# Full-width Z C v, one output pass for two batches, transposes by DMA and a laid-out gate in a Nystrom attention and gating kernel

## The chip, the cores and the metric

The kernel runs on one core of a Trainium2 chip. The metric is the device time of one execution in microseconds, taken several times; the "span" in a profile is the time from the first to the last instruction of the profiled execution, some 1.7 us less. For a program on one core "slow" says only that a run was more than 1.5% above the fastest run of the same kernel on that chip, so it also marks kernels whose own time varies.

## The reference

Eight batches of an attention with 32 landmarks per head, then a gated long convolution on the 512 channels.

```python
B, H, S, D = 8, 8, 576, 64;  m = 32
q_lm = q.reshape(B, H, m, S // m, D).mean(axis=3)
k_lm = k.reshape(B, H, m, S // m, D).mean(axis=3)
A = sm(q, k_lm); Bm = sm(q_lm, k_lm); C = sm(q_lm, k)      # softmax of scaled scores
Z = Bm^T / (norm1(Bm) * norminf(Bm) + 1e-6)
for _ in range(6): Z = 2 * Z - Z @ Bm @ Z
x = (A @ Z @ C @ v)                                        # then heads side by side
proj = x @ w_proj;  x1, x2, x3 = thirds of proj
y = x1 * irfft(rfft(x2) * rfft(filter)) * x3
out = y @ w_out
```

## The kernel before

A batch passes through six parts, each written as a generator: `front` (landmarks, the small matrix), `turns` (k and q turned so that the head dimension lies on partitions), `inverse` (six Newton steps), `back` (scores, exponentials, A, C v, Z C v), `gate` (DFT, filter, inverse DFT, products) and `project` (times w_out, and out). The parts that the argument needs:

```python
def turns(b):                       # batches 0 and 1: on TensorE
    ...
    mm(pt[:, u * R:(u + 1) * R], ..., ident[:R, :R], is_transpose=True, ...)
    (nc.scalar.copy if i == 1 else nc.vector.tensor_copy)(dst[...], pt[:, 0:8 * R])

def inverse(b):
    if b >= NPE:                    # NPE = 2: from batch 2 on by DMA, on the SP queue
        for src, dst in zip((kn, qn), tbufs[b % 2]):
            nc.sync.dma_start_transpose(dst[...], src[...])
    ...

def back(b):
    ...
    A = big.tile([R, NC, 256], F16, tag="A", name="A", bufs=1)
    ...
    for g in range(2):              # A turned on TensorE, evicted by VectorE
        pt = ktile("ptA", F16)
        for c in range(NC):
            mm(pt[:, c * R:(c + 1) * R], A[:, c, 128 * g:128 * g + 128],
               identh[:R, :R], is_transpose=True, start=True, stop=True)
        nc.vector.tensor_copy(AT[:, g, :], pt[:, :S])

def project(b):
    for i0 in range(0, 512, P):     # four passes of 128 rows
        po = wtile()
        for j in range(4):
            mm(po, y[:, j, i0:i0 + P], wout[:, j, :], start=(j == 0), stop=(j == 3))
        os = big.tile([P, Dm], F32, tag="os", name="os", bufs=4)
        nc.scalar.copy(os, po)
        store(i0, P, os)            # nc.sync.dma_start: the SP queue as well
        yield
    po = wtile()                    # the last 64 rows, in two column halves
    ...
    o2 = big.tile([P, 256], F32, tag="o2", name="o2", bufs=1)
    nc.vector.tensor_copy(o2, po[:, 0:256])
    ...                             # two stores
```

`tag` names a pool of `bufs` buffers: a tile waits until the oldest user of its pool is done. The steps of `project` of one batch are done inside the next batch's gate. Loads are issued by GpSimd on a queue of its own (they cast from float32).

The softmax here doesn't subtract the row's maximum and nothing guards it: scores larger than these inputs give would overflow.

## Time and profile before

The median of the runs was 240.9 us (three runs). I mark the start of each batch's gate by its first DFT matmul and name the time from one to the next "gate 0", "gate 1" and so on.

| window, us | to gate 0 | gate 0 | gate 1 | gate 2 | gate 3 | gate 4 | gate 5 | gate 6 | gate 7 and end |
|---|---|---|---|---|---|---|---|---|---|
| before | 33.7 | 32.2 | 28.8 | 25.7 | 24.3 | 24.5 | 22.8 | 21.2 | 28.3 |

A row of the windows view gives the stretch, its length, each engine's busy time with its number of instructions in brackets, and last the granted TensorE clock, the share of the DMA engines in use (it can pass 1, as below) and GB/s. The prediction shows these rows; TensorE is busy 99.5% of a steady window. One more row of that view will matter, gate 2 of the kernel before:

```profile
94.79:120.50 25.71, 25.50 (x330) 15.58 (x327) 21.91 (x56) 21.93 (x51) 3.65 (x5) 1.00 1.39 164
```

The DMA share of 1.39 says that the transfers are crowded there, and still TensorE is busy 25.5 of 25.7 us: nothing waits for them.

### The profile page before, as it was taken

What the parts mean: (1) busy time and instruction counts of PE and PEld (TensorE: products, weight loads), DVE (VectorE), ACT (ScalarE), POOL (GpSimd) and SP (SyncE); (2) the same over time, 40 slices, a digit from 0 to 9 for tenths busy, and PEclk for the clock granted to TensorE, in tenths of its full rate; (3) what the DMA queues carried; (4) which work ended last, traced back from release to release, by engine and by line L of the source; (5) the groups of instructions that cost most, each with busy time, mean ns of one, the idle gap of its engine ahead of it and who ended that gap; (6) DMA issues with size and microseconds to landing.
All of it is one profiled execution on the core that took longest, in us unless ns stands there. A gap on an engine that the chain in (4) does not pass through costs nothing.

```text
span 241.6 us, 6421 instructions
## 1 busy us (share of the span) xinstructions
PE 223.4 (92%) x2547; PEld 134.6 (56%) x2547; DVE 182.4 (75%) x478; ACT 185.8 (77%) x407; POOL 37.7 (16%) x62
## 2 busy tenths in 40 slices
PE   7959769999999999999999999999999999999980
PEld 3537434666665667645754576457645664554630
DVE  8936943579978989896879777977797789567540
ACT  8663525888879878888878888788878987898850
POOL 7962310012203321040032001100000000000000
PEclk9967965999999999999999999999999999999998
DMA  5999999949999999999999996995015004305115
GB/s 73 195 210 196 208 202 198 172 80 176 165 149 167 218 196 154 177 191 146 171 217 140 165 230 152 115 157 173 3 47 152 0 3 107 89 4 150 48 42 153
DMA packets 61998, 33.78 MB, mean 140 GB/s; under 512 B 42320, under 2 KB 57680, under 8 KB 61968
## 3 DMA queue, kind: packets, MB, share of 16 engines
q0 software_dynamic: 27536, 16.85, 53.7%
q1 hardware_dynamic: 34432, 16.52, 36.1%
q8 instruction: 20, 0.33, 0.6%
q14 instruction: 10, 0.08, 0.1%
HBM read 33.69 MB, written 9.44 MB: 178 GB/s over the span
## 4 chain that ended last, share of the span: by engine, by line
PE 78%; DVE 9%; ACT 9%; issue 1%; DVEq 0%; ACTq 0%
PE w L612 12%; PE w L680 11%; PE w L639 6%; PE w L568 6%; PE w L537 6%; PE w L547 5%; PE pc L385 4%; PE pv L421 4%; PE pn L362 3%; PE w L641 3%; PE pq L257 2%; PE ptA L460 2%; PE w L504 2%; PE w L583 2%; PE pk L247 2%; ACT EO L643 2%
## 5 line engine op out<-in xcount | busy, mean ns | idle before, releaser
L680 PE MATMUL w<-wout,y 128*128 128x512 bf16 x128 | 33.4, 380 | 0.4 <-DVE y L658 0.4
L612 PE MATMUL w<-AT,G 128*128 128x512 f16 x128 | 32.8, 380 | 0.2
L541 ACT CAST G<-w 128x512 bf16<-128x512 f32 x48 | 25.5, 597 | 4.0 <-PE w L537 3.9
L617 DVE TENSOR_TENSOR gt<-w,x 128x512 bf16<-128x512 f32 x32 | 21.6, 685 | 9.0 <-ACT x L615 5.0
L643 ACT CAST EO<-w 128x288 bf16<-128x288 f32 x64 | 24.1, 403 | 2.8 <-PE w L641 2.8
L682 ACT COPY os<-w 128x512 f32<-128x512 f32 x32 | 18.5, 589 | 8.9 <-PE w L680 8.3
L639 PE MATMUL w<-IV,Y 128*128 128x288 f16 x128 | 25.0, 286 | 0.3 <-ACT EO L643 0.3
L573 DVE TENSOR_TENSOR T<-X,HH 128x2048 bf16<-128x2048 bf16 x16 | 19.5, 1220 | 7.1 <-ACT X L570 6.4
L615 ACT CAST x<-w 128x512 bf16<-128x512 f32 x32 | 19.0, 599 | 2.9 <-PE w L612 2.4
L537 PE MATMUL w<-wproj,ZC 128*64 128x512 bf16 x96 | 19.4, 400 | 0.0
L547 PE MATMUL w<-F,AE 96*128 96x304 f16 x96 | 19.2, 313 | 0.1
L680 PEld LDWEIGHTS <-y 128*128 128x128 bf16 x128 | 11.0, 97 | 14.5 <-issue 4.2
L570 ACT CAST X<-w 128x512 bf16<-128x512 f32 x32 | 17.9, 592 | 1.4 <-PE w L568 0.9
L396 DVE TENSOR_REDUCE rA<-eA 96x16 f32<-96x512 bf16 x24 | 16.2, 677 | 3.0 <-ACT eA L388 2.8
L641 PE MATMUL w<-IV,Y 128*128 128x288 f16 x64 | 18.3, 286 | 0.0
L568 PE MATMUL w<-G,Ah 128*128 128x512 bf16 x64 | 18.0, 382 | 0.0
L612 PEld LDWEIGHTS <-G 128*128 128x128 bf16 x128 | 11.0, 97 | 12.5 <-ACT G L541 4.0
L366 ACT CAST RZ<-pn 128x256 f16<-128x256 f32 x40 | 15.4, 386 | 2.8 <-PE pn L362 1.8
L96 POOL DMA_DIRECT2D vb<-in_v_dram x16 | 10.8, 678 | 41.0 <-PE w L547 25.1
L549 ACT CAST Ah<-w 128x304 f16<-128x304 f32 x32 | 12.8, 421 | 4.3 <-PE w L547 4.2
L362 PE MATMUL pn<-RZ 128*128 128x160 f16 (+1 forms) x96 | 13.7, 223 | 2.3 <-DVE RZ L367 1.7
L729 PE MATMUL w<-zero 128*128 128x512 bf16 (+1 forms) x55 | 14.2, 398 | 1.4 <-DVE zero L138 1.4
(152 smaller groups left out, 472.4 us busy)
## 6 DMA issues: line engine op xcount, KB each, us to landing
kn<-in_k_dram POOLq DMA_DIRECT2D x8, 576.0 KB, 9.7
qn<-in_q_dram POOLq DMA_DIRECT2D x16, 288.0 KB, 11.5
vb<-in_v_dram POOLq DMA_DIRECT2D x16, 288.0 KB, 9.7
out_dram<-os SPq DMA_DIRECT2D x24, 192.0 KB, 2.5
out_dram<-os SPq DMA_DIRECT2D x16, 128.0 KB, 2.4
wproj<-in_moe_w_proj_dram POOLq DMA_DIRECT2D x3, 512.0 KB, 14.8
out_dram<-os SPq DMA_DIRECT2D x24, 64.0 KB, 2.1
out_dram<-o SPq DMA_DIRECT2D x16, 64.0 KB, 2.1
```

The source lines that it names most:

```text
L362: mm(pn2[:, g, lo:160], RZ[:, g, 0:128], RZ[:, g, lo:160], start=True, stop=True, skip_group_check=True)
L537: mm(pg[64 * pp:64 * pp + 64, :], part["ZC"][:, 2 * g + pp, :, :].rearrange("p h l -> p (h l)"), wparts[jb][:, 2 * g + pp, :], start=True, ...
L541: nc.scalar.copy(G[:, g, Dm * jb:Dm * (jb + 1)], pg)
L547: mm(pf[:, 0:TW], part["AE"][:, par, c, 128 * g:128 * g + 128], F[:, c, par, :], start=(c == 0), stop=(c == 2))
L568: mm(px, Ah[:, g, par, 128 * t:128 * t + 128], G[:, g, Dm:2 * Dm], start=(g == 0), stop=(g == 1))
L573: nc.vector.tensor_tensor(T, X.unsqueeze(2).to_broadcast([P, 2, 2, Dm]), HH[:, par], op=ALU.mult)
L612: mm(px, G[:, g, lo:lo + P], part["AT"][:, g, 0:512], start=(g == 0), stop=(g == 1))
L617: nc.vector.tensor_tensor(gt[:, j, 0:512], px, x1, op=ALU.mult)
L639: mm(pi[:, 0:HS], Y[:, par, t, P * j:P * j + P], IV[:, par, t, :], start=(t == 0), stop=False)
L641: mm(pi[:, 0:HS], Y2[:, P * (j % 2):P * (j % 2) + P], IV2[:, j // 2, par, :], start=False, stop=True)
L643: nc.scalar.copy(EO[:, par, j % 2], pi[:, 0:HS])
L680: mm(po, y[:, j, i0:i0 + P], wout[:, j, :], start=(j == 0), stop=(j == 3))
```

## The change

The intent is to take work off TensorE and to lay the rest out so that it never stands. Z C v comes out at full width because each head's C v has a zero half beside it; G is then made of eight small matmuls on 64x32 tiles, not four on 128x64. The tail frequencies and the last 64 output rows lose their column tiling (two batches share one pass). A's transposes, and those of batch 1's k and q, go to the DMA. The gate is woven in two phases with the side work at fixed places, and the tables are made between the steps of the first front.

```diff
-    NPE = 2
+    NPE = 1                       # k, q on TensorE for batch 0 only
+    NPA = 1                       # A on TensorE for batch 0 only
...
-        A = big.tile([R, NC, 256], F16, tag="A", name="A", bufs=1)
+        A = big.tile([R, 2, NC, P], F16, tag="A", name="A", bufs=1)
...
+        AT = big.tile([P, 2, S], F16, tag="AT", name="AT")
+        if b >= NPA:
+            nc.sync.dma_start_transpose(
+                AT.rearrange("p g (c r) -> p (g c) r", r=R), A.rearrange("p g c l -> p (g c l)"))
...
+            for pos in range(4):
+                for g in range(2):
+                    mm(pg[g][32 * pos:32 * pos + 32, :], part["ZC"][64 * g:64 * g + 64, pos, :],
+                       wparts[jb][64 * g:64 * g + 64, head(g, pos) // 2, :],
+                       start=True, stop=True, skip_group_check=True)
...
-        o2 = big.tile([P, 256], F32, tag="o2", name="o2", bufs=1)
-        nc.vector.tensor_copy(o2, po[:, 0:256])
+        if b % 2 == 1:
+            yl = lasts.pop(b // 2)
+            po = wtile()
+            for j in range(4):
+                mm(po, yl[:, j].rearrange("p e s -> p (e s)"), wout[:, j, :],
+                   start=(j == 0), stop=(j == 3))
+            o2 = big.tile([P, Dm], F32, tag="os", name="o2", bufs=4)
+            nc.vector.tensor_copy(o2, po)
...
+        for b in range(2, B):
+            g = gate(b, pending)
+            todo = [(g, 7, 0, 1)]
+            if b + 1 < B: todo.append((K_[b + 1], 9, 0, 1))
+            if b + 2 < B: todo.append((F_[b + 2], 8, 0, .9))
+            turns_dma(b + 2)
+            weave(*todo, end=False); run(*[(x[0], ALL) for x in todo[1:]])
+            vload(b + 2)
+            todo = [(g, 17, 0, 1)]
+            if b + 2 < B: todo += [(E_[b + 2], 6, 0, .9), (I_[b + 2], 6, 0, 1)]
+            weave(*todo)
+            loads(b + 3)
+            pending = project(b)
```

(The cuts leave out the layout of the tail tables, the zero halves, the start and the order of heads.)

## The prediction

> **What bounds the kernel now.** I read the page first, then cut the span into batches, then asked for the chain of waits inside one batch. The page:
>
> ```profile
> PE 223.4 (92%) x2547; PEld 134.6 (56%) x2547; DVE 182.4 (75%) x478; ACT 185.8 (77%) x407; POOL 37.7 (16%) x62
> PEclk9967965999999999999999999999999999999998
> DMA  5999999949999999999999996995015004305115
> PE 78%; DVE 9%; ACT 9%; issue 1%; DVEq 0%; ACTq 0%
> ```
>
> TensorE is busy 92% of 241.6 us and holds 78% of the chain that ended last. Averages mix the start with the steady part, so I marked where each batch's gate begins, by the first DFT matmul (line 547) of each, and asked for the windows between these marks:
>
> ```profile
> core 0: us, PE busy (x) PEld busy (x) DVE busy (x) ACT busy (x) POOL busy (x), PEclk, DMA share, GB/s
> 0.00:65.97 65.97, 56.10 (x626) 34.71 (x627) 47.49 (x145) 43.29 (x89) 23.14 (x42) 0.87 1.18 171
> ...
> 120.50:144.83 24.33, 24.13 (x291) 14.31 (x289) 19.44 (x51) 20.62 (x47) 3.64 (x5) 1.00 1.25 190
> 144.83:169.32 24.49, 24.36 (x298) 14.80 (x295) 19.76 (x52) 20.94 (x48) 1.33 (x2) 1.00 0.89 149
> ...
> 213.32:241.60 28.28, 21.08 (x154) 10.77 (x151) 12.86 (x23) 17.62 (x38) 0.00 (x0) 0.97 0.31 84
> ```
>
> In the steady batch TensorE is busy 24.36 of 24.49 us; ScalarE has 20.94 (86%), VectorE 19.76 (81%). So a steady batch is TensorE's, but ScalarE stands only 3.5 us below. The start is different: 65.97 us for one batch, with a granted clock of 0.87 and no engine full. Its chain runs through VectorE making the sine table (1.4 to 12.3 us), a table load on ScalarE, then a ladder of short steps.
>
> The rows that the change touches:
>
> ```profile
> L537 PE MATMUL w<-wproj,ZC 128*64 128x512 bf16 x96 | 19.4, 400 | 0.0
> L462 DVE COPY AT<-ptA 128x576 f16<-128x576 f16 x16 | 7.2, 447 | 3.9 <-PE ptA L460 3.9
> ...
> L583 PE MATMUL w<-G,Ah 128*32 128x256 bf16 x128 | 5.8, 276 | 0.0
> L688 PE MATMUL w<-wout,y 128*64 128x256 bf16 x64 | 5.4, 274 | 0.0
> ```
>
> Durations overlap here, so I took the time in the chain: in the batch from 142.7 to 167.2 us the chain gives line 537 8.2% of 24.49 us (2.0 us for 12 matmuls), line 583 2.2% (0.54 us for 16), line 460 2.1% (0.51 us for 12). Full matmuls of 512 columns stand at 0.86 us for four there, 215 ns each.
>
> **What the Trainium skill says.** "TensorE: Matmul & The Clock Gate", section "Back-to-back issue gap", gives N/2.4 + 2.5 ns for a warm matmul alone, 216 ns at N = 512. The trace agrees: 215 ns. The same page, "Part 3: Packing small matmuls", has small tiles in different row and column strips run side by side (nine tiles 6.32 times as fast as one by one). The trace shows it for columns alone: 16 matmuls of 256 columns on 32-wide tiles take 0.54 us where one by one would be 16 x 109 ns = 1.7 us. Rows and columns at once it does not show. "TensorEngine Tiling (Array Packing)", section "Key Properties", says that a change of tiling mode drains the engine: the four matmuls of line 537 stand at 0.55 us or more in the chain against 2 x 216 ns = 0.43. "VectorE: DVE Perf Modes", section "The three transpose paths", gives 390 ns on TensorE and 1309 ns by DMA for a 128x128 block, but TensorE pipelines: here twelve 96-column transposes take 0.51 us of chain, and the DMA's time is beside it.
>
> **The change, part by part, on TensorE in one steady batch.**
> 1. The transposes of A go to the DMA (all batches but the first): -0.51 us, and two VectorE copies, -0.89 us there.
> 2. G from ZC: four matmuls on 128x64 tiles become eight on 64x32 tiles, eight places at once. Ideal is one pass of 216 ns; with a drain and eight starts I take 0.40 us (an estimate) in place of 2.0/3 = 0.67 us. Three such parts: -0.8 us.
> 3. The tail frequencies: 16 tiled matmuls become two full ones, 2 x 0.216 = 0.43 against 0.54: -0.11 us. VectorE loses one instruction, line 592, 285 ns.
> 4. The last 64 rows: 8 half-width matmuls per batch (ideally 4 x 109 = 0.44 us, x64 in the row above) become 4 full ones per pair of batches, 0.43 us a pair: -0.22 us.
> 5. ZC wants 8 matmuls in place of 4 (about 30 ns each): +0.12. DFT tables are 320 wide, not 304: 12 x 16 / 2.4 = 80 ns: +0.08.
> Sum: -0.51 - 0.8 - 0.11 - 0.22 + 0.2 = -1.44 us, so 24.49 becomes about 23.05 us. ScalarE keeps all its evictions (20.9 us, 91% of that), so it should not bind yet, but half of its slack is gone. VectorE: -0.89 - 0.29 - 0.13 (ZC copy half as large) + 0.07 (y in two pieces) = 18.5 us.
>
> **The start.** Batch 1's k and q are no longer turned on TensorE: 48 transposes of 96 columns (2 us) and six evictions of 0.55 to 0.8 us leave the window before 66 us. The tables are made between the steps of the front, with the two constants and ScalarE fills after them put later: the first lm copy starts at 15.7 us now, while q arrives for the matmul at 10.5 us; I give 3 us for that. Batch 0 gets parts 2 to 5 (0.9 us), batch 1's back part 1. With the second half of gate 0 woven through batch 1's scores, inverse and batch 2's front, I estimate 1 us more. Together 65.97 becomes about 58.5 us.
>
> **The sum by windows** (now, then): to gate 1, 65.97, 58.5. Gate 1, 28.82, 27.5. Gate 2, 25.71, 24.0. Gates 3 and 4, 24.33 and 24.49, each 23.0. Gate 5, 22.80, 23.0, because the front of batch 7 is now done here, not earlier. Gate 6, 21.20, 18.7 (the scores of batch 7 have moved into gate 5). Gate 7 and the end, 28.28, 26.5 (-1.4 of TensorE, and ScalarE has 17.6 there, so nearly all counts). New total: 58.5 + 27.5 + 24.0 + 23.0 + 23.0 + 23.0 + 18.7 + 26.5 = 224.2 us of span. Span and measured median agree within 1 us before (241.6 and 240.9), so I say **224 us**, -7%.
>
> **Rivals.**
> *The DMA becomes the bound.* Its queues tell what moves:
>
> ```profile
> q0 software_dynamic: 27536, 16.85, 53.7%
> q1 hardware_dynamic: 34432, 16.52, 36.1%
> ...
> kT<-kn SPq DMA_TRANSPOSE x6, 10.9
> qT<-qn SPq DMA_TRANSPOSE x6, 9.3
> ```
>
> Before: 33.78 MB. Added: two transposes of 0.59 MB for batch 1 and seven of A, half as large each: 1.18 + 2.06 = 3.2 MB. Loads alone run at 202 GB/s (window 20 to 38 us), transposes alone at about 185 (46 to 50 us). 37.0 MB at 190 GB/s are 195 us of 224. For this rival: a steady batch moves 3 x 0.59 + 2 x 0.59 + 0.29 + 1.18 = 4.4 MB in 23 us, 192 GB/s, about what the DMA gives; and the stores wait in the same queue as the transposes, in order. Against it: now the last load is issued at 150 us with DMA share under 0.25 after 169 us, so there is slack at the end, and no compute engine waits for a transfer longer than 0.2 us after the start. If it holds, a batch costs 25 us and the total is 230 to 238.
> *ScalarE becomes the bound.* 20.94 us per batch plus small gaps is 21.5 to 22; TensorE at 23.05 is above. It binds only in gate 1, with two batches of exponentials: part of why I take only 1.3 us off there. If the weave puts evictions badly, a batch stays at 24: total 229.
> *The small tiles don't overlap.* If rows and columns together gave no more than columns do now, eight matmuls of 512 columns on four places cost 0.43 + 0.1 us and the gain of part 2 falls from 0.8 to 0.4 us: 227. If they ran one by one, 8 x 216 = 1.73 us, +3.2 us per batch and no gain at all: 249. The tiled matmuls in the trace speak against the last.
> *Better than counted.* TensorE's streaming columns in a batch sum to some 22.6 us by my count, so 1.9 us are stalls and drains; a weave that takes away half of them and a start that never drops to half clock (0.50 at 38 to 40 us) would give 214 to 217, where ScalarE stops it.
>
> **Range and chances.** 224, with 214 to 234 for 8 in 10: below lies the better weave, above the DMA or ScalarE. Faster by over 2% means under 236.1 us; only a saturated DMA or serial tiles take the result there. Faster 0.91, same 0.07, slower 0.02.
>
> **What would show it.** Steady gates 23 us apart with TensorE over 97% busy: the sum is right. TensorE under 93% with ScalarE over 95%: ScalarE binds. Waits of scores or of the factor matmuls on kT, qT or AT of many us: the DMA. G's matmuls: eight in under 0.45 us of chain, or not. The first lm copy near 12.5 us, and gate 1 near 58 us: the start is right. The prediction fails if DMA transposes land too late for the scores of batches 1 and 2, where loads still fill the engines, or if the woven order makes TensorE, which runs in order, stand behind an eviction.

## The result

The changed kernel took 254.8 us in the median of four runs (253.7 to 256.6) beside 242.4 for the kernel before: slower, with a ratio of 1.055 (95% interval 1.042 to 1.068). Ratios here are the mean time of one kernel's fast runs over that of the other's fast runs of the same rounds, so they are not quite the ratio of the medians. The predicted 224 us with its range of 214 to 234 was wrong, and on the wrong side of the kernel before.

The page of the changed kernel, the lines that answer to the first four of the prediction, and the row of TensorE's busy share:

```profile
PE 209.2 (82%) x2369; PEld 125.1 (49%) x2369; DVE 172.6 (68%) x460; ACT 185.4 (73%) x411; POOL 38.0 (15%) x62
PE   7868699179499699919139999999999999999990
PEclk9999889959979999976858999999999999999997
DMA  6999999999999899999992999989205203604116
PE 37%; DMA 29%; DVE 12%; ACT 11%; SPq 3%; issue 3%; POOL 2%; DVEq 0%; ACTq 0%
```

TensorE has 14 us less to do, as meant, but the chain that ended last is no longer TensorE's: 29% of it are transfers, which the same line of the kernel before does not list at all. The granted clock is at 5 to 7 tenths only in and just after the slices in which TensorE was busy for 1 to 4 tenths; the longest such stretch lies just before the middle of the span. The windows:

| window, us | to gate 0 | gate 0 | gate 1 | gate 2 | gate 3 | gate 4 | gate 5 | gate 6 | gate 7 and end |
|---|---|---|---|---|---|---|---|---|---|
| predicted | 58.5 for both | | 27.5 | 24.0 | 23.0 | 23.0 | 23.0 | 18.7 | 26.5 |
| after | 29.7 | 40.4 | 28.4 | 42.5 | 22.6 | 23.2 | 22.0 | 18.1 | 28.1 |

```profile
29.66:70.08 40.42, 30.00 (x381) 18.99 (x382) 24.95 (x77) 24.09 (x52) 4.43 (x6) 0.87 1.35 176
98.44:140.93 42.49, 27.57 (x308) 16.60 (x304) 22.42 (x59) 22.75 (x52) 3.63 (x5) 0.80 1.11 165
140.93:163.55 22.62, 21.70 (x281) 13.37 (x277) 18.76 (x50) 20.11 (x47) 3.65 (x5) 1.00 1.30 176
163.55:186.71 23.16, 22.41 (x286) 13.70 (x282) 19.43 (x51) 20.34 (x47) 1.33 (x2) 1.00 0.65 142
```

From gate 3 on the windows lie within 1.6 us of the prediction. The whole miss sits in two windows. Gate 0 ends at 70.1 us, not 58.5: 11.6 us. Gate 2 lasts 42.5 us, not 24: 18.5 us. Together 30.1 us, and 224.2 + 30.1 is 254.3; the span was 254.9. In both windows no engine is near full, so they are made of waits.

The waits of the changed kernel in gate 0 (who waited for whom: total us, times, longest):

```profile
PE pc L410 <- DMA qT<-qn: 8.9, 2, 6.7
```

and in gate 2 (some lines are left out):

```profile
DVE o L719 <- DMA out_dram<-os: 10.8, 1, 10.8
...
PE pn L386 <- DVE RZ L391: 9.4, 1, 9.4
...
DVE A L442 <- DMA AT<-A: 5.8, 1, 5.8
```

In gate 0 the scores of batch 1 wait 6.7 us for qT, now made by DMA, and those of batch 2 wait 2.3 us. In gate 2 VectorE first waits 5.8 us to write A, because the transpose that reads A's only buffer has not finished. Then it waits 10.8 us to write `o`, the last rows of two batches, because the pool of four `os` buffers has none free: a store has not landed. TensorE's 9.4 us are VectorE's wait handed on, since the Newton step that it needs stands behind that copy on VectorE, which did nothing else meanwhile. Why the store is late is seen on the SP queue (start, us, issue):

```profile
103.94 3.45 SPq L448 DMA_TRANSPOSE AT<-A  x1
107.55 3.21 SPq L360 DMA_TRANSPOSE qT<-qn  x1
110.87 7.14 SPq L360 DMA_TRANSPOSE kT<-kn  x1
118.10 1.00 SPq L700 DMA_DIRECT2D out_dram<-os  x2
119.20 5.98 SPq L448 DMA_TRANSPOSE AT<-A  x1
125.27 3.46 SPq L700 DMA_DIRECT2D out_dram<-os  x6
```

ScalarE had filled the first `os` buffer by 104 us. Its store was issued at 118.1 us, after A's transpose of batch 2 and both transposes of batch 5 (the fifth pair in the queue, of which batch 1's is the first; some of the expectations below call it batch 4's), and landed at about 129.4 us, when the chain lets VectorE go. Of the 25.4 us, 14.1 lie before the issue. The rest, 10.7 us to land for the last piece, is long too: the medians of such stores are 2.6 to 3.8 us by size. Batch 5's transposes were ahead of it on the same queue, and its kT landed at 127.4 us.

### The profile page after: what moved, and what is told of

It is laid out like the page before. It is cut to its first block, busy times and chain, and to the rows that moved or that the text cites. A ratio compares the mean times of both kernels' runs of the same rounds, so it can differ in the third digit from the quotient of the medians.

```text
span 254.9 us, 6078 instructions
## 1 busy us (share of the span) xinstructions
PE 209.2 (82%) x2369; PEld 125.1 (49%) x2369; DVE 172.6 (68%) x460; ACT 185.4 (73%) x411; POOL 38.0 (15%) x62
## 4 chain that ended last, share of the span: by engine, by line
PE 37%; DMA 29%; DVE 12%; ACT 11%; SPq 3%; issue 3%; POOL 2%; DVEq 0%; ACTq 0%
DMA qT<-qn 15%; PE w L707 6%; PE w L636 5%; DMA AT<-A 5%; DMA out_dram<-os 5%; PE w L575 5%; DMA kn<-in_k_dram 4%; PE w L663 4%; SPq L360 3%; PE pc L410 2%; ACT EO L667 2%; DVE T L606 2%; PE w L665 2%; PE w L564 2%; PE w L601 2%
## 5 line engine op out<-in xcount | busy, mean ns | idle before, releaser
L636 PE MATMUL w<-AT,G 128*128 128x512 f16 x128 | 34.8, 380 | 2.8 <-DMA AT<-A 2.2
L663 PE MATMUL w<-IV,Y 128*128 128x288 f16 x128 | 27.1, 301 | 0.0
L667 ACT CAST EO<-w 128x288 bf16<-128x288 f32 x64 | 24.2, 411 | 2.6 <-PE w L665 2.1
L568 ACT CAST G<-w 128x512 bf16<-128x512 f32 x48 | 25.1, 605 | 0.6 <-PE w L564 0.6
L709 ACT COPY os<-w 128x512 f32<-128x512 f32 x32 | 18.7, 595 | 8.4 <-PE w L707 8.4
L390 ACT CAST RZ<-pn 128x256 f16<-128x256 f32 x40 | 15.8, 394 | 10.9 <-PE pn L386 10.8
L413 ACT ACTIVATE eA<-pc 96x512 bf16<-96x512 f32 x24 | 15.0, 624 | 12.0 <-PE pc L410 12.0
L386 PE MATMUL pn<-RZ 128*128 128x160 f16 (+1 forms) x96 | 14.1, 229 | 11.4 <-DVE RZ L391 11.0
L639 ACT CAST x<-w 128x512 bf16<-128x512 f32 x32 | 19.7, 617 | 3.5 <-PE w L636 3.1
L707 PEld LDWEIGHTS <-y 128*128 128x128 bf16 x128 | 11.9, 99 | 15.8 <-issue 2.9
L575 PE MATMUL w<-F,AE 96*128 96x320 f16 x96 | 17.5, 325 | 2.1 <-DVE AE L475 2.1
L665 PE MATMUL w<-IV,Y 128*128 128x288 f16 x64 | 19.2, 300 | 0.0
L410 PE MATMUL pc<-lm,qT 128*128 128x64 bf16 x192 | 11.0, 201 | 9.7 <-DMA qT<-qn 8.9
L83 POOL DMA_DIRECT2D kn<-in_k_dram x8 | 6.5, 815 | 74.6 <-PE pk L269 28.1
L386 PEld LDWEIGHTS <-RZ 128*128 128x128 f16 x96 | 8.5, 98 | 17.9 <-issue 13.6
L601 PE MATMUL w<-G,Ah 128*128 128x512 bf16 x64 | 16.7, 380 | 0.0
L98 POOL DMA_DIRECT2D vb<-in_v_dram x16 | 10.8, 677 | 39.4 <-PE pv L458 33.2
## 6 DMA issues: line engine op xcount, KB each, us to landing
qn<-in_q_dram POOLq DMA_DIRECT2D x16, 288.0 KB, 12.5
```

The lines of the kernel that those rows point to most:

```text
L386: mm(pn2[:, g, lo:160], RZ[:, g, 0:128], RZ[:, g, lo:160], start=True, stop=True, skip_group_check=True)
L568: nc.scalar.copy(G[:, g, Dm * jb:Dm * (jb + 1)], pg[g])
L575: mm(pf[:, 0:TW], part["AE"][:, par, g, c, :], F[:, c].rearrange("p a x -> p (a x)")[:, TW * par:TW * par + TW], start=(c == 0), stop=(c = ...
L601: mm(px, Ah[:, g, o:o + P], G[:, g, Dm:2 * Dm], start=(g == 0), stop=(g == 1))
L636: mm(px, G[:, g, lo:lo + P], part["AT"][:, g, 0:512], start=(g == 0), stop=(g == 1))
L639: nc.scalar.copy(x1, px)
```

## The experiments

Twelve kernels ran. I began with two theories. **A, order:** single waits in the one in-order queue that carries stores and transposes. **B, bytes:** the transfers are at their limit until gate 3, so only the megabytes count. B looked good at first: from the windows (length times GB/s) the kernel before had moved 20.7 MB when its gate 3 began at 120.5 us, the changed one 24.3 MB at 140.9 us, and 3.6 MB at 180 GB/s are the 20 us of delay. After four runs I formed a third: **C**, two separate losses, batch 1's transposes in gate 0, and the shared output buffer behind a blocked queue in gate 2. The windows of all runs' profiled executions:

| kernel | to gate 0 | gate 0 | gate 1 | gate 2 | gate 3 | gate 4 | gate 5 | gate 6 | span |
|---|---|---|---|---|---|---|---|---|---|
| before | 33.7 | 32.2 | 28.8 | 25.7 | 24.3 | 24.5 | 22.8 | 21.2 | 241.6 |
| changed | 29.7 | 40.4 | 28.4 | 42.5 | 22.6 | 23.2 | 22.0 | 18.1 | 254.9 |
| e1 | 29.7 | 32.4 | 32.8 | 36.8 | 22.6 | 23.2 | 22.0 | 18.1 | 245.8 |
| e2 | 30.7 | 36.3 | 26.3 | 41.5 | 22.9 | 23.7 | 22.4 | 18.6 | 250.4 |
| e3 (slow) | 30.8 | 32.4 | 26.5 | 38.1 | 22.9 | 23.7 | 22.4 | 18.6 | 243.5 |
| e4 | 30.8 | 40.9 | 28.1 | 30.1 | 22.6 | 23.2 | 22.0 | 18.1 | 244.0 |
| e5 | 30.7 | 32.4 | 26.5 | 25.6 | 22.9 | 24.5 | 22.3 | 18.6 | 231.5 |
| e6 | 29.7 | 32.4 | 26.0 | 31.1 | 22.6 | 23.2 | 22.0 | 18.1 | 233.3 |
| e7 | 29.7 | 39.8 | 28.5 | 43.1 | 22.6 | 23.2 | 22.0 | 18.1 | 255.0 |
| e8 (slow) | 33.7 | 32.2 | 28.8 | 38.9 | 34.1 | 24.5 | 22.8 | 21.2 | 264.6 |
| e9 (slow) | 30.6 | 30.8 | 32.3 | 24.0 | 22.6 | 24.1 | 22.0 | 18.1 | 232.8 |
| e10 | 30.6 | 40.4 | 34.0 | 31.2 | 22.6 | 24.3 | 22.0 | 18.1 | 251.3 |
| e11 | 29.7 | 39.8 | 28.5 | 25.1 | 31.7 | 26.4 | 28.0 | 18.6 | 255.8 |
| e12 (slow) | 30.5 | 30.8 | 30.0 | 25.6 | 28.3 | 24.2 | 22.0 | 18.1 | 237.4 |

### e1: batch 1's k and q back on TensorE

```diff
-    NPE = 1
+    NPE = 2
-        weave((g, 2, 0, 1), (F_[1], 5, 0, 1), end=False); run((F_[1], ALL))
+        weave((g, 2, 0, 1), (F_[1], 5, 0, 1), (U_[1], 6, 0, 1), end=False)
+        run((F_[1], ALL), (U_[1], ALL))
```

> The changed kernel with batch 1's k and q turned on TensorE again (48 transposes, 6 evictions), all else as changed. Theory A, single waits in the order of one DMA queue: the scores of batch 1 stood 6.7 us before qT and those of batch 2 some 6 us more because the transposes of batch 2 queue behind those of batch 1; both go, TensorE gets 2 us back: about -10 us, 245 us, and the gate of batch 1 starts near 60 us, not 70. Theory B, bytes: until gate 3 the transfers are at their limit of some 180 GB/s and only the bytes count: 1.18 MB fewer is -6.5 us, +2 us of TensorE: 250 us.

Measured: 248.4 us, ratio 1.033, between the 245 of A and the 250 of B. Gate 0 fell from 40.4 to 32.4 us, so 8 us of the loss are this one choice, although TensorE has its 48 transposes back. Gate 1 then grew by 4.4 us: its factor matmuls now waited 5.3 us for A's transposed copy. A wait taken away let the next one show.

### e2: A back on TensorE

```diff
-    NPA = 1
+    NPA = 8
```

> The changed kernel with all transposes of A on TensorE again. Theory A (order): the waits on A's transfer in gates 1 and 2 (2.2 us of factor matmuls, 5.8 us of VectorE, and the stores that stood behind A's transpose of batch 3 while VectorE waited 10.8 us for their buffer) go: -15 us, plus 0.5 us per batch for the transposes: 243 us, gate 2 under 30 us, not 42.5. Theory B (bytes): 0.9 MB fewer before gate 3 is -5 us, and +3.5 us: 253 us.

Measured: 252.0 us, ratio 1.045. Theory A missed: gate 2 stayed at 41.5 us with no transpose of A in the queue at all. VectorE waited even longer for the store, 14.7 us, and the queue says why:

```profile
107.39 3.36 SPq L360 DMA_TRANSPOSE qT<-qn  x1
110.85 3.29 SPq L360 DMA_TRANSPOSE kT<-kn  x1
114.23 7.30 SPq L700 DMA_DIRECT2D out_dram<-os  x8
```

The stores still stood behind batch 5's transposes, which themselves came only when the load of batch 5's q had landed; the queue's own list of waits has 6.8 us for that. The total is what B had said, but B's reason fails with the next runs.

### e3: both back on TensorE

The edits of e1 and e2 together, main lines only.

```diff
-    NPE = 1
-    NPA = 1
+    NPE = 2
+    NPA = 8
```

> The changed kernel with both back on TensorE: the transfers of the kernel before under the changed order and the changed matmuls. Theory A (order): all three stalls go, 30 us less and 5 us of TensorE more: 228 to 230 us, under the kernel before by 5%. Theory B (bytes): 2.1 MB fewer before gate 3, -11.5 us and +5: 248 us. A third theory, that the woven order itself is bad: it stays over 245 us with TensorE waiting on evictions.

Measured: 245.0 us in the median; one run, 240.1 us, counts as fast. A and B both missed; the third theory's number is near the slow runs, but TensorE did not wait on evictions. The bytes are those of the kernel before (33.76 MB beside 33.78), and gate 2 still took 38.1 us. Its waits in the profiled run, which was a slow one:

```profile
DVE o L719 <- DMA out_dram<-os: 14.9, 2, 11.3
```

In gate 2 one long wait of VectorE remained, 11.3 us for an output buffer. This is where theory C came from. It is no matter of slow runs alone: e2's fast run has the same wait, and e5 takes it away.

### e4: the last rows' output in a buffer of its own

```diff
-            o2 = big.tile([P, Dm], F32, tag="os", name="o2", bufs=4)
+            o2 = big.tile([P, Dm], F32, tag="o2", name="o2", bufs=1)
```

The local memory is full, so `Y2` and `yl`, which are used once per batch or pair, went from two buffers to one.

> The changed kernel with one buffer of its own for the output of the last rows (room for it from one buffer less of two small tiles that are used once per batch). Theory A (order and buffers): VectorE no longer stands 10.8 us on a store in gate 2: -8 us, 247 us. Theory B (bytes): the next wait takes the place of this one, and it stays within 2 us of the changed kernel, 253 to 256 us.

Measured: 245.7 us for the fast run, the profiled one, and 250.4 to 251.9 for three that count as slow. In this one profile gate 2 fell from 42.5 to 30.1 us with every byte unchanged, and gate 0 stayed at 40.9. B can't give that; e5 and e8 confirm the buffer as the cause. What was left in gate 2 is the wait on A's buffer (5.4 us).

### e5: both on TensorE, and the own buffer

The edits of e3 and e4 together, of which only the main lines are shown.

```diff
-    NPE = 1
-    NPA = 1
+    NPE = 2
+    NPA = 8
-            o2 = big.tile([P, Dm], F32, tag="os", name="o2", bufs=4)
+            o2 = big.tile([P, Dm], F32, tag="o2", name="o2", bufs=1)
```

> Batch 1's k and q and all of A turned on TensorE, and the output of the last rows in a buffer of its own. New theory C: two separate losses, 8 us before gate 1 from batch 1's transposes sent by DMA among the loads, and 11 us in gate 2 where VectorE waits for a store that stands in the queue behind the transposes of batch 4. The run with both on TensorE still had the second (11.3 us in its trace, gate 2 of 38.1 us). C: gate 2 falls to 26 to 27 us and the span from 243.5 to 232; the ratio to before is 0.96 to 0.97. If bytes set it (theory B), another wait takes its place and it stays at 240 or more.

Measured: 232.6 us (231.4 to 233.3, all fast), ratio 0.966 (0.959 to 0.973): theory C's number. Gate 2 of this kernel in the windows view, to be set beside the row of the changed kernel above:

```profile
89.60:115.16 25.56, 24.91 (x330) 15.87 (x329) 23.74 (x63) 22.44 (x52) 3.64 (x5) 1.00 1.36 150
```

The DMA share is 1.36, as crowded as in the kernel before, and TensorE is busy 24.9 of 25.6 us. Crowded transfers cost this kernel next to nothing, since nothing stood waiting for them.

### e6: batch 1 on TensorE, the own buffer, A by DMA

The edits of e1 and e4 together, main lines only.

```diff
-    NPE = 1
+    NPE = 2
-            o2 = big.tile([P, Dm], F32, tag="os", name="o2", bufs=4)
+            o2 = big.tile([P, Dm], F32, tag="o2", name="o2", bufs=1)
```

> Batch 1's k and q on TensorE, A by DMA as in the change, the last rows' output in its own buffer. C: the wait of gate 1 on A's transposed copy (5.3 us) and that of VectorE on A's buffer in gate 2 (5.4 us) stay, the store wait goes: gates 0 to 2 last 32.4, 32.8 and about 30 us, span 239. Later gates 22.6, 23.2, 22.0, 18.1 as in the changed kernel, 0.5 us each under those with A on TensorE.

Measured: 236.2 us, ratio 0.980 (0.973 to 0.987). Gate 2 at 31.1 us is as expected; gate 1 came out at 26.0, not 32.8, without the wait on A's copy. Against e4 only batch 1's transposes differ, and gate 0 goes from 40.9 to 32.4. So with both runs, e1 and e6, those transposes by DMA cost 8 us. And B is refuted once more: 1.18 MB fewer should be 6.5 us, but gate 3 starts at 119.2 us here, 21.7 us sooner than in the changed kernel. Gates 3 to 6 are those of the changed kernel, 22.6, 23.2, 22.0 and 18.1 us, 0.2 to 1.3 us under e5's, which is what A by DMA is worth there; the loads end in these gates.

### e7: the transposes after the stores, by program order

```diff
-            turns_dma(b + 2)
             weave(*todo, end=False); run(*[(x[0], ALL) for x in todo[1:]])
+            turns_dma(b + 2)
```

> The changed kernel with one thing moved: from gate 2 on, the transposes of batch b + 2 enter the queue after the first half of the gate, so behind the stores of that gate and not ahead of them. Buffers and bytes as in the change. C (the queue's order makes the store late): VectorE's wait on the store in gate 2 falls from 10.8 us to under 2; the transposes now come later, so the scores of batch 4 may wait for qT, up to 8 us; span between 244 and 254. If the store is late for lack of bandwidth, the wait of VectorE stays near 10 us.

Measured: 256.9 us, ratio 1.064, all windows within 0.7 us of the changed kernel's. This experiment failed as an experiment: the order of the queue is set when the program is scheduled, and the queue in e7's trace shows the same order of transposes and stores in gate 2 as before the edit (kT at 110.2 us, the first store at 117.6). It told nothing of C and served as a repeat of the changed kernel.

### e8: the kernel before, with the shared pool alone

```diff
-        o2 = big.tile([P, 256], F32, tag="o2", name="o2", bufs=1)
+        o2 = big.tile([P, Dm], F32, tag="os", name="o2", bufs=4)[:, 0:256]
```

> The kernel before with that one part of the change: the output of the last rows takes its buffer from the pool of four that the other output rows use. C: in the kernel before, too, the stores of the second project stood behind a transpose (106.5 to 114.5 us in its trace), so VectorE should come to wait on a store there: 3 to 9 us, 244 to 250 us. If the shared buffer hurts only under the woven order: 240 to 242 us.

Measured: one fast run of 259.1 us and three slow ones of 266 to 268, beside 239.7 to 242.4 for the fast runs of the kernel before. I had expected 3 to 9 us and got at least 16.7 (259.1 less 242.4). Nothing else is different, neither the weave nor the bytes. From the slow profiled run, the waits between 94 and 168 us, and the queue:

```profile
DVE o L692 <- DMA out_dram<-os: 20.4, 2, 11.5
```

```profile
102.19 3.76 SPq L353 DMA_TRANSPOSE qT<-qn  x1
106.05 7.67 SPq L353 DMA_TRANSPOSE kT<-kn  x1
113.81 6.83 SPq L673 DMA_DIRECT2D out_dram<-os  x8
```

The queue is as in the kernel before:

```profile
106.47 8.07 SPq L353 DMA_TRANSPOSE kT<-kn  x1
114.64 6.68 SPq L673 DMA_DIRECT2D out_dram<-os  x8
```

There, too, eight stores stood behind kT until 114.6 us, and nobody minded, because four `os` buffers hold four tiles. With a fifth user in each batch VectorE waits 11.5 us in gate 2 and 8.9 us in gate 3. So the late store is old; the change made something wait for it.

### e9: A in two buffers

On top of e6:

```diff
-        A = big.tile([R, 2, NC, P], F16, tag="A", name="A", bufs=1)
+        A = big.tile([R, 2, NC, P], F16, tag="A", name="A", bufs=2)
-        AE = big.tile([R, 2, 2, 3, P], F16, tag="AE", name="AE")
+        AE = big.tile([R, 2, 2, 3, P], F16, tag="AE", name="AE", bufs=1)
```

> Batch 1's k and q on TensorE, A transposed by DMA, the last rows' output in its own buffer, and A in two buffers (room from AE, which gets one). C: the 5.5 us that VectorE waits in gate 2 for A's buffer to be read by its transpose go, gate 2 falls from 31.1 to about 25.6 us, the later gates stay 22.6, 23.2, 22.0, 18.1: span 227 to 229, ratio to before 0.94 to 0.955, and faster than the version with all of A on TensorE (231.5). If one buffer of AE hurts, the later gates grow by 0.5 us each.

Measured: 234.5 us in the median, fast runs 233.9 and 230.9, ratio 0.964 (0.955 to 0.973). The profiled run was a slow one. Gate 2 is 24.0 us there, so the wait on A's buffer is gone as expected. Gate 1, though, lasts 32.3 us, with a wait of 4.7 us for A's copy as in e1, and 7.4 us of VectorE waiting for the matmuls of a later batch's landmarks. The expected gain over e5 did not come; what gate 1 was in the fast runs isn't known.

### e10: loads of batch 2 held back

From e4, GpSimd reads one column of batch 1's kT and qT before it issues the loads of batch 2.

```diff
-    loads(2); turns_dma(1)
+    turns_dma(1)
+    held = consts.tile([P, 2], BF16, name="held")
+    for i in range(2):
+        nc.gpsimd.tensor_copy(held[:, i:i + 1], tbufs[1][i][:, 24 * R - 1:24 * R])
+    loads(2)
```

> The changed kernel with the last rows' output in its own buffer (that run is the one to compare with: gate 0 of 40.9 us, span 244) and the loads of batch 2 held back until the transposes of batch 1 have landed. If the loads that share the transfer engines made those transposes late (qT landed 22 us after its issue), qT lands some 8 to 10 us earlier, and the 6.7 us that the scores of batch 1 waited go; what is held back then comes late, so the scores of batch 2 wait longer, and the end of gate 0 need not gain: gate 0 between 37 and 42 us. If qT was late for another reason (its own issue), the first wait stays at 6 us or more.

Measured: 253.3 us, ratio 1.051. The copy that waits for qT ran here

```profile
L795 POOL COPY held<-qT x1: 188/188/188, 44.3 to 44.3; 128x1 bf16<-128x1 bf16 x1
```

at 44.3 us, where the changed kernel's scores got qT at 52.3 us. Both issued it at 30.0 us. So the loads that shared the engines made it 8 us late. But gate 0 still lasted 40.4 us: now the scores of batch 2 waited 6.6 us for their qT, and gate 1 grew from e4's 28.1 to 34.0 us. It looks as if in gate 0 the sum of loads and transposes counts, as theory B says. This one run doesn't show it, since holding the loads back made the transposes of batch 2 late by itself (kT issued at 52.2 us, not 45.4).

### e11: the transposes after the stores, pinned

The move of e7, with the transposes from batch 4 on tied behind whatever was traced before them on the queue; the built program shows them behind the stores.

```diff
-                nc.sync.dma_start_transpose(
+                x = nc.sync.dma_start_transpose(
                     ...)
+                if b >= 4: tc.keep_in_program_order(x)
```

> The earlier attempt to move the transposes behind the stores did not change the queue at all: its order is set when the program is scheduled. Here the transposes from batch 4 on are pinned behind what was traced before them in the queue, so behind the stores of their gate; buffers and bytes as in the changed kernel. C (the place in the queue makes the store late): VectorE's wait on the store in gate 2 falls from 10.8 us to under 3; the scores of batch 4 may now wait up to 8 us for qT; span 243 to 254. If it is bandwidth: VectorE still waits near 10 us.

Measured: 257.8 us, ratio 1.068. The queue in gate 2:

```profile
103.40 0.79 SPq L701 DMA_DIRECT2D out_dram<-os  x2
104.65 1.31 SPq L449 DMA_TRANSPOSE AT<-A  x1
106.05 4.62 SPq L701 DMA_DIRECT2D out_dram<-os  x6
```

The first store goes out at 103.4 us, not 118.1; VectorE's wait for a buffer left gate 2's list of waits (one of 3.6 us remains elsewhere), and gate 2 fell from 42.5 to 25.1 us with the shared pool in place. So the place in the queue made the store late. The first pieces also landed within 2.2 us, not 10.7; the edit took transposes out of the stretch as well, so for these 8.5 us it doesn't tell the queue from the crowding. Alone they would have left a wait of about 2 us (an estimate: 103.8 + 10.7 us against VectorE's copy at 112.5). The span, 255.8 us, missed the expected 243 to 254. The price is in this line of the waits, over the whole run:

```profile
PE pc L411 <- DMA qT<-qn: 19.9, 6, 6.4
```

Transposes that are issued late are waited for in gates 3 to 5 (31.7, 26.4 and 28.0 us). Neither of the two orders tried served both stores and transposes in time.

### e12: A by DMA from batch 4 on

On top of e6:

```diff
-    NPA = 1
+    NPA = 4
```

> What the runs point to: batch 1's k and q and A of batches 0 to 3 on TensorE while loads fill the transfer engines, A of batches 4 to 7 by DMA, the last rows' output in its own buffer. C: gates 0 to 2 as with all of A on TensorE (32.4, 26.5, 25.6 us), gates 3 to 6 as with A by DMA (22.6, 23.2, 22.0, 18.1): span 229 to 231, ratio to before 0.95 to 0.965, about 1 us under the version with all of A on TensorE. If A's transposes are free of harm only by chance there, a later gate grows and it ends at 232 or more.

Measured: 233.4 us in the median of seven runs (fast ones 231.3 to 233.4), ratio 0.965 (0.959 to 0.971), at the top of the expected ratio. The spans of the fast runs are 229.6 to 231.7 us, where 229 to 231 was expected, and not under e5's (229.7 to 231.6), so the gain over e5 did not show. The profiled run was a slow one: gate 1 lasted 30.0 us (26.5 expected) and gate 3 28.3 (22.6 expected), so a later gate did grow there; its fast runs have no trace, and I leave open whether it grew in them. e5, e9 and e12 take some 3.5% less time than the kernel before, and their intervals overlap: I can't tell them apart (by its class alone, e5's gain is "unclear"). e5 had no slow run among its four, the other two had some.

## Why the prediction was wrong

**The TensorE sum came out, with some luck.** It said 24.49 - 1.44 = 23.05 us for a steady gate, and 22.6 and 23.2 came out, with ScalarE at 20.1 to 20.3 us, below. But TensorE's busy time fell by 2.4 and 2.0 us, not 1.44, while its idle time grew from 0.1 to 0.2 us up to 0.8 to 0.9: two misses that nearly cancel. By the prediction's own sign, over 97% busy, it fell just short (96% and 97%). In the last window TensorE's work fell by 0.4 us, not 1.4. The one term with no evidence in the trace, G on 64x32 tiles, held: eight matmuls took 0.34 us of chain where 0.40 was guessed.

```profile
165.94 0.34 PE w L564 x8
```

**"The start" had its sign wrong.** The text took 2 us and six evictions off for batch 1's transposes and set no cost against it. Its last sentence names the danger, transposes that land too late for the scores of batches 1 and 2 while loads fill the engines, but the sum has no term for it. They cost 8 us (e1, and e6 against e4). The early part of it held partly: the lm copy starts at 14.2 us, not 15.7 (12.5 was foretold), and gate 0 starts at 29.7, not 33.7. e5, with those transposes back on TensorE, ends gate 0 at 63.1 us, so without the DMA's loss the estimate of 58.5 would still have been 4.6 us short, of which 2 us are the transposes. (The sum is one of spans; measured times are some 1.7 us above, which the prediction took for equal.)

**Part 4 was counted as matmuls only.** The step "The last 64 rows: 8 half-width matmuls per batch ... become 4 full ones per pair of batches, 0.43 us a pair: -0.22 us" is the one that failed most. The diff's line with `tag="os"` was in plain sight: in every second batch five tiles through four buffers, the fifth written by VectorE, in order, ahead of Newton steps. In place of a gain of 0.22 us a batch, the runs showed a wait of VectorE for a buffer: 12.4 us in gate 2 (42.5 against 30.1 in e4), and 16.7 us or more in the kernel before (e8).

**The DMA rival was named and then argued away.** It even says that the stores wait in the same queue as the transposes. But it was sized by megabytes per batch, which is not what happened (e6), and dismissed because the kernel before waited for no transfer and had slack at the end of its span. Both were true and neither answered the question. Slack at the end can't be used in gates 0 to 2, where the loads of k for batches 3 to 6 are issued (42.4 to 109.6 us). And a trace without waits says that nothing needed those transfers yet, not that they were early: their stores stood behind a transpose for 8 us already. The Trainium skill's "DMA: Bandwidth & Descriptors", section "Anatomy of one DMA — SWDGE (gpsimd) path", has half of what was overlooked: DMA engines do not wait on semaphores, the wait happens on the issuing sequencer before dispatch. e2's trace agrees: the queue stood from 100.4 to 107.4 us until a load had landed, and the stores behind it stood too. The changed kernel shows the other half: batch 5's loads had landed by 100.6 us, and from 103.9 to 118.1 us the queue was filled by the issuing of three transposes alone, 3.45 + 3.21 + 7.14 us. The same page, section "Queues, rings and completion order", says that an engine takes turns between the queues it has work for; e10 fits that, with 8 us between a qT that shared with loads and one that shared with fewer, but no run shows the turns themselves.

**A's transposes** were counted as 0.51 us gained with their DMA time "beside it". From gate 3 on that held (e6 against e5). Before, they cost some 5 us more in gate 2, through A's single buffer (e6's 31.1 us against 25.6 in e5; in e9 a second buffer brought 24.0, in a slow run).

**The losses don't add.** e2 removed A's transposes and won 1 us of gate 2; e4 removed the buffer and won 12.4; together with batch 1's they won 17. Each wait hides those that would end sooner. What stays open is why gate 1 lasts 26.0 us in e6 and 32 to 33 in e1 and e9: the trace shows the wait on A's copy there, and one link behind it. A's transpose of batch 1 stands in the queue behind batch 3's, which follow a load of q that GpSimd issued at 60.9 us in e1, 59.4 in e9 and 56.9 in e6; A's transposes went out at 74.8, 73.4 and 68.0 us. Why that load was later is not shown.

## What to carry to other kernels

When work moves to a DMA queue, ask what else is in that queue, what each entry waits for before it is issued, and who needs what stands behind it; a transfer nobody waits for today is no proof that it is early. When a tile joins a pool, count the users per round against the buffers, and ask which engine will stand in order behind the one that comes too many. A loss made of waits is taken apart by windows, not by totals: removing one wait alone (e2) told almost nothing here until the other was gone.

## What the Trainium skill lacked or had wrong

- "DMA: Bandwidth & Descriptors" gives rates for DMA transposes, but none for one that shares the engines with loads. Here the same transpose of a 96x3072 tile of bf16 landed between 5.6 and 22.3 us after its issue:

```profile
DMA to landing us min/median/max: 5.6/9.2/22.3
```

- "VectorE: DVE Perf Modes", section "The three transpose paths", compares 390 ns on TensorE with 1309 ns by DMA for one 128x128 block. Many blocks in one instruction cost less: 24 blocks of 96x128 in 5.6 us are 233 ns each, and on TensorE twelve took 0.51 us of chain, 43 ns each, without the two copies out (0.89 us on VectorE). The single-block figures don't choose between the paths; here the queue did.
- "TensorE: Matmul & The Clock Gate", "Part 3: Packing small matmuls", has no row for 64x32 tiles. Eight matmuls of 512 columns took 0.34 us of chain, where eight one by one at 216 ns would take 1.73 us: a factor of 5.
- "DMA: Bandwidth & Descriptors" has no time for which issuing a transpose of these sizes holds the queue, and doesn't say what that does to stores behind it. Here issuing qT took 2.4 to 14.2 us and A's transpose 1.3 to 6.0 us; a store ready at 104.0 us went out at 118.1 us, and one at 103.4 us when the transposes were put behind it. No run tried stores and transposes on two queues.
